# Output weights in longer runs, mixed earlier, and other cuts of three loads, in a decode layer of attention and a dense block

## The chip, the cores and the metric

The kernel runs on one core of one Trainium2 chip. The metric is the device time of one execution in microseconds (us), lower is better; the median of seven executions is given. A core has TensorE (PE, matrix products into PSUM; PEld is its weight load), VectorE (DVE), ScalarE (ACT), GpSimd (POOL), SyncE (SP, which here only issues loads) and 16 DMA engines between HBM and SBUF. Each engine runs its own list of instructions in order and waits on semaphores.

## The reference

One decode step for two sequences. `x` is normalised; attention of 16 query heads over 8 key/value heads looks at the last 4096 cached positions; a dense block with the mish activation stands beside it; both are added to `x`.

```python
B, Sq, D = 2, 1, 448;  Hq, Hkv, Sk, Dh = 16, 8, 32768, 256;  F = 1792
xn = layernorm(x)
q = (xn @ wq) as 16 heads;  k, v = caches[:, :, Sk - 4096:, :], each for two query heads
p = softmax(q . k * Dh ** -0.5);  attention = (p @ v) as one row of 4096 @ wo
h = xn @ w1 + b1;  act = h * tanh(log(1 + exp(h)))
out = x + attention + act @ w2
```

All is bf16. The caches that are read hold 2 x 8 x 4096 x 256 elements each, 33.6 MB for keys and as much for values; the weights are wq 3.7 MB, wo 3.7 MB, w1 and w2 1.6 MB each. Nothing is read twice: some 77.7 MB in all.

## The kernel before

The order of instructions on every engine is the order of the program (a manual schedule); the framework adds the semaphores. SP issues all the large loads, in program order on one DMA queue. ACT issues x and b1 at the start on another queue.

The work is in four units `u`. A unit has four pairs (sequence, key/value head), `J = 4`, and its keys and values come in four loads each, `k(u, r)` and `v(u, g)`, 128 partitions of 16384 bytes (2 MB). Three buffers hold keys, four hold values (wq and w1 use the value buffers first, w2 a key buffer at the end). `load_wo(u)` (L104) brings the unit's output weights, 0.92 MB, as two loads with runs of 1792 bytes. The framework gives loads eight completion semaphores in turn, so a load also waits for the one eight places before it.

For a unit, DVE turns each key load (`turn`, L243, two transposes of 32x32 blocks a load) into `kt`. When all four are turned, PE makes the scores in two halves (`scores`, L318), ACT takes the exponential, DVE transposes it to `p`; `weigh` (L343) sums it for the denominator; `values` (L365) multiplies p with the value loads into `pv`; `gather` (L379, L385) copies `pv` to SBUF and sums its parts by fixed selection matrices; `finish` (L412) divides and leaves `oT`, the attention output with the head dimension on partitions, two columns (the sequences) for each of four heads and two halves. `mix(u)` multiplies oT with wo and adds to the accumulator `acc`: 8 groups of rows, each as four products of 112 columns into four groups of PSUM rows (`add_rows`, L223). In the loop `mix(u - 1)` stands after `weigh(u)`.

`acc` holds the sum of everything: it begins with x (L212), gets the mixes of four units and the dense block's second product (`dense_out`, also through `add_rows`). Query projection, the dense block's first product (`dense_in`, L443) and `mish` run ahead of the loop. In the last unit the loads are, in SP's order: wo(3), v(3,0) to v(3,2), v(3,3) in two parts of 24 and 8 tokens a partition, and w2 in three parts: its first half, then 5 rows and 2 rows of 7 of the second half (a row is 448 numbers a partition). The last value load takes another way, straight into the gathered sum (`values_fixed`, L400). After the last w2 part come its products, four copies out of acc (L559, L561) and the store of the result.

Of the kernel before, what the change touches and what calls it, by code (L numbers as in the profile page):

```python
# [11 lines left out]
BF16 = mybir.dt.bfloat16  # L12
FP32 = mybir.dt.float32
PSUM = bass.MemoryType.PSUM
# [3 lines left out]
def kernel(  # L18
# [27 lines left out]
    KU = J // Bsz  # L46
    U = Hkv // KU
    C = P // J
    CT = W // C
    T = CT // R  # L50
# [8 lines left out]
    NI = F2 // P  # L59
    DG = D // G  # L60
# [11 lines left out]
    consts = ctx.enter_context(tc.tile_pool(name="consts", bufs=1))  # L72
    small = ctx.enter_context(tc.tile_pool(name="small", bufs=2))
# [2 lines left out]
    ps_o = ctx.enter_context(tc.tile_pool(name="ps_o", bufs=1, space=PSUM))  # L76
    ps_den = ctx.enter_context(tc.tile_pool(name="ps_den", bufs=1, space=PSUM))
    ps_a = ctx.enter_context(tc.tile_pool(name="ps_a", bufs=1, space=PSUM))
    ps_m = ctx.enter_context(tc.tile_pool(name="ps_m", bufs=2, space=PSUM))

    KE = T * Dh
    kview = A_k_cache.rearrange("b (k u) s d -> u (b k) s d", u=U)
# [2 lines left out]
    def ring(name):  # L85
        return v_pool.tile([P, KE], BF16, tag="v", name=name)

    k_t, v_t, wo_t = {}, {}, {}

    def load_k(u, r):  # L90
        t = k_pool.tile([P, KE], BF16, tag="k", name="k")
        src = kview[u][:, s0:, :].rearrange("j (c t) d -> c j (t d)", c=C)
        nc.sync.dma_start(out=t[:], in_=src[:, :, r * KE : (r + 1) * KE])  # L93
        k_t[u, r] = t

    def load_v(u, g, lo=0, hi=T):
        if lo == 0:
            v_t[u, g] = ring("v")
        t = v_t[u, g]
        src = vview[u][:, s0:, :].rearrange("j (g x t) d -> g x j (t d)", g=G, x=C)  # L100
        nc.sync.dma_start(  # L101
            out=t[:, lo * Dh : hi * Dh], in_=src[g, :, :, lo * Dh : hi * Dh]
        )

    def load_wo(u):
        w = wo_pool.tile([P, KU, rep, 2 * D], BF16, tag="wo", name="wo")
        for k2 in range(KU):
            r0 = (u + U * k2) * rep * Dh
            nc.sync.dma_start(  # L109
                out=w[:, k2, :, :],  # L110
                in_=A_wo[r0 : r0 + rep * Dh, :].rearrange("(h p c) d -> p h (c d)", h=rep, p=P),
            )
        wo_t[u] = w

    x_bf = consts.tile([Bsz, D], BF16)
    nc.scalar.dma_start(out=x_bf[:, :], in_=A_x.flatten_outer_dims())
    b1_sb = consts.tile([P, 2, NI], BF16)
    nc.scalar.dma_start(out=b1_sb[:], in_=B_b1.rearrange("(k q c) -> q k c", k=2, q=P))

    load_k(0, 0)  # L120
    load_k(0, 1)
# [2 lines left out]
    for lo, hi in ((0, 4), (4, NS)):  # L124
        t = ring("wq")
# [4 lines left out]
    ident = consts.tile([P, P], BF16)  # L130
# [2 lines left out]
    nc.gpsimd.memset(qd[:], 0.0)  # L133
    ones = consts.tile([P, P], BF16)
    nc.gpsimd.memset(ones[:], 1.0)
    eps_t = consts.tile([Bsz, 1], FP32)
    nc.vector.memset(eps_t[:], 1e-5)

# [6 lines left out]
        out=rstd[:], in_=mv[:, 1:2], func=ACT.Sqrt, bias=eps_t[:], scale=1.0  # L145
# [4 lines left out]
        out=xn_bf[:],  # L150
# [8 lines left out]
        out=parm[:], in_=ident[:].rearrange("p (a o) -> p o a", o=2), axis=AXIS.X, op=ALU.add  # L159
# [3 lines left out]
        out=jm[:],  # L163
        in_=ident[:].rearrange("p (a j h) -> p j a h", j=J, h=rep),
# [4 lines left out]
        out=jm[:], in0=jm[:], scalar1=-1.0, scalar2=29952.0, op0=ALU.add, op1=ALU.mult  # L169
# [3 lines left out]
        out=mneg[:], in_=jm[:].unsqueeze(1).to_broadcast([P, TH * 8, J])  # L173
    )
    sel = consts.tile([P, 2, NQ], FP32)
    for x in range(2):
        for w in range(4):
            at = 32 * w + (2 * (w % 2) + x) * NQ
            src = ident[:, at : at + NQ]
            if w == 0:  # L180
                nc.vector.tensor_copy(out=sel[:, x, :], in_=src)
            else:
                nc.vector.tensor_tensor(
                    out=sel[:, x, :], in0=sel[:, x, :], in1=src, op=ALU.add
                )

    xr_ps = ps_m.tile([P, NS, Bsz], BF16, tag="m", name="xr_ps")
    xn_v = xn_bf[:].rearrange("b (a k) -> b a k", k=NS)
    for s in range(NS):
        r = s // 2  # L190
        step = 3 + s % 2
        xrow = consts.tile([Bsz, P // 2, 2], BF16, name=f"xrow{s}")
        nc.vector.tensor_copy(out=xrow[:], in_=xn_v[:, :, r : r + step + 1 : step])  # L193
        nc.tensor.transpose(  # L194
            xr_ps[:, s, :], xrow[:].rearrange("b a o -> b (a o)"), ident[0:Bsz, 0:Bsz]
        )
    xs = consts.tile([P, NS, 32], BF16)
    nc.gpsimd.memset(xs[:], 0.0)
    for odd in range(2):
        for half in range(2):  # L200
            o = (half + odd) % 2
            nc.vector.tensor_scalar(
                out=xs[:, odd::2, half * Bsz : (half + 1) * Bsz],
# [3 lines left out]
                op0=ALU.mult,  # L207
            )

    acc = ps_a.tile([P, DG], FP32)  # L210
    for g in range(G):
        nc.tensor.matmul(  # L212
            acc[32 * g : 32 * (g + 1), :],
            lhsT=ident[0:Bsz, 0:32],
            rhs=x_bf[:, g * DG : (g + 1) * DG],
            start=True,
            stop=False,
            skip_group_check=True,
        )

    def add_rows(lhsT, rows, stop=False):
        for g in range(G):
            nc.tensor.matmul(  # L223
                acc[32 * g : 32 * g + Bsz, :],
                lhsT=lhsT,
                rhs=rows[:, g * DG : (g + 1) * DG],
                start=False,
                stop=stop,
                skip_group_check=True,
            )  # L230
# [74 lines left out]
    def scores(u, i):  # L305
        sc = ps_sc.tile([P, TH, 32], FP32, tag="sc", name="sc")
        nc.tensor.matmul(  # L307
            sc[:].rearrange("p t m -> p (t m)"),
            lhsT=ident[:],
            rhs=mneg[:].rearrange("p a j -> p (a j)"),  # L310
            start=True,
            stop=False,
            skip_group_check=True,
        )
        for n in range(NB):
            for e in range(2):
# [16 lines left out]
        nc.vector.transpose(  # L333
            out=p_t[i][:].rearrange("p g t q -> p t g q"),
            in_=ex[:].rearrange("p t (g q) -> p t g q", g=G),
        )

    state = {}
# [70 lines left out]
    def finish(u):  # L409
# [8 lines left out]
        )  # L418
        state["oT", u] = oT

    def mix(u):
        oT, w = state.pop(("oT", u)), wo_t.pop(u)
        for k2 in range(KU):
            for h in range(rep):
                for c in range(2):
                    add_rows(oT[:, c, k2 * rep + h, :], w[:, k2, h, c * D : (c + 1) * D])
# [47 lines left out]
        nc.vector.tensor_tensor(out=t_sb[:], in0=t_sb[:], in1=den[:], op=ALU.mult)  # L474
        nc.vector.tensor_tensor(out=act_bf[:], in0=h_sb[:], in1=t_sb[:], op=ALU.mult)

    w2_parts = ((0, 0, NI), (1, 0, 5), (1, 5, NI))

    def load_w2(part):
        if part == 0:  # L480
            state["w2"] = k_pool.tile([P, KE], BF16, tag="k", name="w2")
        k, lo, hi = w2_parts[part]
        w2_in = B_w2.flatten().rearrange("(k p e) -> k p e", k=2, p=P)
        at = k * NI * D
        nc.sync.dma_start(
            out=state["w2"][:, at + lo * D : at + hi * D],
            in_=w2_in[k, :, lo * D : hi * D],
        )
# [9 lines left out]
    def turns(u, r):  # L498
        for i in range(NH):
            turn(u, r, i)  # L500
# [10 lines left out]
    for u in range(U):  # L511
        last = u == U - 1
        if last:
            load_wo(u)
        load_v(u, 0)
        load_v(u, 1)
        load_v(u, 2)
        if last:
            load_v(u, 3, 0, 24)
            load_v(u, 3, 24, T)  # L520
            for part in range(3):
                load_w2(part)
        else:
            load_v(u, 3)
            load_k(u + 1, 0)
            load_k(u + 1, 1)
            load_k(u + 1, 2)
            load_wo(u)
            load_k(u + 1, 3)
        scores(u, 0)  # L530
        scores(u, 1)
        weigh(u)
        if u > 0:
            mix(u - 1)
        for g in range(G - 1):
            values(u, g)
        if not last:
            values(u, G - 1)
            turns(u + 1, 0)
            turns(u + 1, 1)  # L540
            gather(u)
            finish(u)
            turns(u + 1, 2)
            turns(u + 1, 3)
    u = U - 1
# [2 lines left out]
    values_fixed(u, G - 1, 24, T)  # L548
    finish(u)
    mix(u)  # L550
    for part in range(3):
        dense_out(part)

    res = consts.tile([Bsz, D], BF16)
    for g in range(G):
        dst = res[:, g * DG : (g + 1) * DG]
        src = acc[32 * g : 32 * g + Bsz, :]
# [35 lines left out]
```

The softmax here doesn't subtract the row's maximum and nothing guards it: scores larger than these inputs give would overflow.

## Time and profile before

| What | us |
|---|---|
| median of 7 executions (lowest, highest) | 193.06 (192.77, 193.27) |
| the profiled execution | 193.09 |
| its span on the core | 191.3 |
| busy: PE / DVE / ACT / POOL | 68.8 / 90.7 / 11.3 / 2.9 |
| key transposes on DVE (L243), 32 | 72.1 |
| PE idle ahead of the scores (L318) | 62.4 |

The span runs from the first instruction to the last; 1.8 us of the execution lie around it. The page divides the span into 40 slices of 4.8 us and gives the busy share of each engine in tenths, so a row of nines is an engine at work throughout. A time to landing is from the issue of a load to its completion semaphore. In a line of a view in order of time the first number is the start, the second the duration in us, and the brackets give how long the engine stood idle before and what ended that. The trace also has a record of every DMA packet (start, duration, size) and of each engine's completion mark for a load, without the number of the engine.

The loads as the page lists them:

```profile
k<-in_A_k_cache_dram SPq DMA_DIRECT2D x16, 2048.0 KB, 27.3
v<-in_A_v_cache_dram SPq DMA_DIRECT2D x15, 2048.0 KB, 23.5
wo<-in_A_wo_dram SPq DMA_DIRECT2D x8, 448.0 KB, 30.5
```

### The profile page before, as it was taken

The numbers are of one execution on the slowest core, as the hardware profiler recorded it, in microseconds if no ns is written. First come the engines' busy times: TensorE is split into PE (matmuls) and PEld (weight loads), VectorE is DVE, ScalarE is ACT, GpSimd is POOL, SyncE is SP. The second block draws the span as 40 slices with busy tenths as digits, with TensorE's granted clock in tenths as the row PEclk, the third lists the DMA queues.
The fourth block names the chain that finished last, engine by engine and source line by source line (L and its number), as shares of the span: only waits on it lengthen the run. The fifth ranks groups of instructions, "written<-read, shape, count | busy, mean of one in ns | idle before, by whom it ended". The sixth has DMA issues, their size and how long they took to land.

```text
span 191.3 us, 2051 instructions
## 1 busy us (share of the span) xinstructions
PE 68.8 (36%) x892; PEld 33.7 (18%) x892; DVE 90.7 (47%) x96; ACT 11.3 (6%) x19; POOL 2.9 (2%) x13
## 2 busy tenths in 40 slices
PE   0201525197336000097234000385262000673492
PEld 0100115032113000033013000132031000231191
DVE  4897066573001998553004995822007994740001
ACT  3000030011001000011000000020010000020101
POOL 6000000000000000000000000000000000000000
PEclk9999999999755555569955555589755555599555
DMA  5999999999999999999999999999999999999980
GB/s 216 405 425 422 434 423 447 418 428 418 435 432 432 421 400 421 438 432 432 418 421 432 435 408 425 421 425 432 432 428 428 406 420 403 437 425 421 413 344 16
DMA packets 8082, 77.80 MB, mean 407 GB/s; under 512 B 1029, under 2 KB 3209, under 8 KB 3593
## 3 DMA queue, kind: packets, MB, share of 16 engines
q1 hardware_dynamic: 7796, 77.66, 96.7%
q8 instruction: 7, 0.11, 0.2%
q10 hardware_dynamic: 276, 0.01, 0.1%
q14 instruction: 3, 0.02, 0.0%
HBM read 77.67 MB, written 0.00 MB: 406 GB/s over the span
## 4 chain that ended last, share of the span: by engine, by line
DMA 86%; DVE 7%; SPq 2%; PE 2%; issue 0%; DVEq 0%
DMA k<-in_A_k_cache_dram 53%; DMA w<-in_B_w_dram 27%; DVE kt L243 7%; DMA wo<-in_A_wo_dram 7%; PE h_ps L443 1%; SPq L93 1%; SPq L126 1%; PE acc L223 0%; SPq L101 0%; DVEq L588 0%; DVE res L559 0%; SPq L109 0%
## 5 line engine op out<-in xcount | busy, mean ns | idle before, releaser
L243 DVE STREAM_TRANSPOSE kt<-k 128x2048 f32<-128x2048 f32 x32 | 72.1, 2290 | 55.8 <-DMA k<-in_A_k_cache_dram 55.8
L318 PE MATMUL sc<-kt,qd 128*32 128x512 bf16 x256 | 22.6, 511 | 62.4 <-DVE kt L243 62.4
L365 PE MATMUL pv<-v,p 128*32 128x512 bf16 x240 | 19.4, 462 | 23.7 <-DMA v<-in_A_v_cache_dram 23.7
L318 PEld LDWEIGHTS <-qd 128*32 128x32 bf16 x256 | 8.7, 117 | 74.5 <-issue 72.4
L365 PEld LDWEIGHTS <-p 128*32 128x32 bf16 x240 | 7.1, 107 | 34.2 <-issue 30.7
L333 DVE STREAM_TRANSPOSE p<-ex 128x512 bf16<-128x512 bf16 x8 | 5.7, 711 | 13.6 <-ACT ex L327 13.6
L327 ACT ACTIVATE ex<-sc 128x512 bf16<-128x512 f32 x8 | 4.8, 597 | 84.7 <-PE sc L318 84.7
L385 PE MATMUL o<-sel,vs 128*128 128x8 f32 x32 | 7.5, 364 | 2.9 <-ACT vs L379 2.9
L385 PEld LDWEIGHTS o<-sel,vs 128*128 128x128 f32 x32 | 7.1, 326 | 6.5 <-ACT vs L379 6.5
L265 PE MATMUL q_ps<-wq,xs 128*32 128x512 bf16 x28 | 3.4, 624 | 12.5 <-DMA wq<-in_A_wq_dram 12.5
L412 DVE TENSOR_TENSOR oT<-o,rec 128x16 bf16<-128x16 f32 x4 | 0.6, 145 | 12.8 <-PE o L400 12.8
L379 ACT COPY vs<-pv 128x512 f32<-128x512 f32 x4 | 2.3, 585 | 49.0 <-PE pv L365 49.0
L343 PE MATMUL dn<-p,ones 128*128 128x512 bf16 x8 | 3.1, 383 | 4.5 <-DVE p L333 4.5
L443 PE MATMUL h_ps<-xs,w 128*128 128x4 bf16 x49 | 2.8, 193 | 5.1 <-DMA w<-in_B_w_dram 5.1
L307 PE MATMUL sc<-mneg,ident 128*128 128x512 bf16 x8 | 4.3, 535 | 0.0
L282 DVE COPY qT<-qt_ps 128x16 bf16<-128x16 bf16 x4 | 0.4, 168 | 6.9 <-PE qt_ps L277 6.9
L351 DVE TENSOR_REDUCE rec<-dn 128x8 f32<-128x512 f32 x4 | 2.8, 691 | 1.9 <-PE dn L343 1.9
L443 PEld LDWEIGHTS <-w 128*128 128x128 bf16 x49 | 2.7, 152 | 5.2 <-DMA w<-in_B_w_dram 5.2
L265 PEld LDWEIGHTS <-xs 128*32 128x32 bf16 x28 | 1.0, 125 | 14.0 <-issue 14.0
L194 PE MATMUL xr_ps<-ident,xrow 2*128 2x2 bf16 x7 | 1.0, 181 | 6.5 <-DVE xrow L193 6.5
L223 PEld LDWEIGHTS <-oT 128*2 128x2 bf16 x128 | 1.8, 91 | 5.5 <-issue 5.1
L223 PE MATMUL acc<-wo,oT 128*2 128x112 bf16 x128 | 2.6, 232 | 0.3 <-DVE oT L412 0.3
(51 smaller groups left out, 28.7 us busy)
## 6 DMA issues: line engine op xcount, KB each, us to landing
k<-in_A_k_cache_dram SPq DMA_DIRECT2D x16, 2048.0 KB, 27.3
v<-in_A_v_cache_dram SPq DMA_DIRECT2D x15, 2048.0 KB, 23.5
wo<-in_A_wo_dram SPq DMA_DIRECT2D x8, 448.0 KB, 30.5
wq<-in_A_wq_dram SPq DMA_DIRECT2D x1, 2048.0 KB, 16.3
w<-in_B_w_dram SPq DMA_DIRECT2D x1, 1568.0 KB, 26.7
wq<-in_A_wq_dram SPq DMA_DIRECT2D x1, 1536.0 KB, 19.3
v<-in_A_v_cache_dram SPq DMA_DIRECT2D x1, 1536.0 KB, 26.8
w<-in_B_w_dram SPq DMA_DIRECT2D x1, 784.0 KB, 23.9
```

Source lines behind the costliest of these rows:

```text
L223: nc.tensor.matmul(acc[32 * g : 32 * g + Bsz, :], lhsT=lhsT, rhs=rows[:, g * DG : (g + 1) * DG], start=False, stop=stop, skip_group_check= ...
L243: nc.vector.transpose(out=kt[i][:, :, :, r, :], in_=t[:, i * w : (i + 1) * w].bitcast(FP32).rearrange("p (a c j) -> p a c j", c=P // (R * ...
L265: nc.tensor.matmul(q_ps[32 * u : 32 * (u + 1), :], lhsT=xs[:, s, :], rhs=wq_t[s][:, u * 512 : (u + 1) * 512], start=(s == 0), stop=(s == N ...
L307: nc.tensor.matmul(sc[:].rearrange("p t m -> p (t m)"), lhsT=ident[:], rhs=mneg[:].rearrange("p a j -> p (a j)"), start=True, stop=False, ...
L318: nc.tensor.matmul(sc[32 * w : 32 * (w + 1), :, :], lhsT=qd[:, u, 2 * n + e, :, :].rearrange("p g q -> p (g q)"), rhs=ktm[i][:, n, e, :, 3 ...
L327: nc.scalar.activation(out=ex[:].rearrange("p t m -> p (t m)"), in_=sc[:].rearrange("p t m -> p (t m)"), func=ACT.Exp, scale=scale,)
L333: nc.vector.transpose(out=p_t[i][:].rearrange("p g t q -> p t g q"), in_=ex[:].rearrange("p t (g q) -> p t g q", g=G),)
L343: nc.tensor.matmul(dn[:].rearrange("p a q -> p (a q)"), lhsT=ones[:], rhs=p_t[i][:].rearrange("p g t q -> p (g t q)"), start=(i == 0), sto ...
L351: nc.vector.tensor_reduce(out=rec[:], in_=dn[:].rearrange("p a q -> p q a"), axis=AXIS.X, op=ALU.add)
L365: nc.tensor.matmul(pv[32 * w : 32 * (w + 1), :, :].rearrange("p x d -> p (x d)"), lhsT=p_t[a // 4][:, g, 4 * (a % 4) : 4 * (a % 4) + 4, :] ...
L385: nc.tensor.matmul(po[:, c, :], lhsT=sb[:, x, c::2], rhs=sel[:, x, :], start=(x == 0 and c == 0), stop=(last and x == 1), skip_group_check ...
L443: nc.tensor.matmul(h_ps[:, i, :, :].rearrange("p k b -> p (k b)"), lhsT=w1_v[:, s, i, :], rhs=xs[:, s, 0 : 2 * Bsz], start=(s == 0), stop= ...
```

## The change

*Output weights of units 0, 1 and 2.* `load_wo` brings them in one load with 7168 bytes a partition: eight successive rows of wo lie on one partition. The unit's 1024 rows are (head group k, head h, row within the head), so a partition now stands for 8 rows of one k and h, and oT no longer fits. `relay(u)` re-lays it: 16 products with constant one-hot matrices (`hot`, made on POOL at the start) bring the 1024 values into a PSUM tile of 128 partitions by 8 rows by 2 sequences; ACT copies it to SBUF as `ox`. `mix_early(u)` then makes 8 products of full width, 448 columns, into a new accumulator `early` that begins with x. Both stand ahead of the scores of the next unit; the `mix` after `weigh` is gone. Before the last unit's scores, `carry` copies `early` to SBUF and starts `acc` from it with four fp32 products. Unit 3 keeps its two loads and `mix`.

*v(3,0).* Its first 26 tokens of each partition's 32 come in one load, the last 6 in four loads of 32 partitions each.

*w2.* Its second half comes in 4, 2 and 1 rows in place of 5 and 2.

*b1.* ACT issues it in five parts of 64, 16, 16, 16 and 16 partitions in place of one.

*Memory.* A PSUM bank goes to `early`, so the pool of small PSUM tiles has one buffer in place of two; the rows of x that are transposed at the start (`xrows`) share a buffer with `ex`.

```diff
-    ps_m = ctx.enter_context(tc.tile_pool(name="ps_m", bufs=2, space=PSUM))
+    ps_e = ctx.enter_context(tc.tile_pool(name="ps_e", bufs=1, space=PSUM))
+    ps_m = ctx.enter_context(tc.tile_pool(name="ps_m", bufs=1, space=PSUM))
...
-    def load_v(u, g, lo=0, hi=T):
+    def load_v(u, g, lo=0, hi=T, x0=0, x1=C):
...
-            out=t[:, lo * Dh : hi * Dh], in_=src[g, :, :, lo * Dh : hi * Dh]
+            out=t[J * x0 : J * x1, lo * Dh : hi * Dh], in_=src[g, x0:x1, :, lo * Dh : hi * Dh]
...
-        for k2 in range(KU):
+        if u < U - 1:
+            nc.sync.dma_start(
+                out=w[:].rearrange("p k h e -> p (k h e)"),
+                in_=A_wo.rearrange("(k u y i) d -> u y k (i d)", k=KU, u=U, i=8)[u],
+            )
+        for k2 in range(KU if u == U - 1 else 0):
...
-    nc.scalar.dma_start(out=b1_sb[:], in_=B_b1.rearrange("(k q c) -> q k c", k=2, q=P))
+    for lo, hi in ((0, 64), (64, 80), (80, 96), (96, 112), (112, P)):
+        nc.scalar.dma_start(out=b1_sb[lo:hi], in_=b1_in[lo:hi])
...
+    early = ps_e.tile([Bsz, D], FP32)
+    nc.tensor.matmul(
+        early[:], lhsT=ident[0:Bsz, 0:Bsz], rhs=x_bf[:], start=True, stop=False
+    )
     acc = ps_a.tile([P, DG], FP32)
...
+    def carry():
+        e_sb = small.tile([P, 2 * Dh], FP32, tag="vs", name="e_sb", bufs=1)[0:Bsz, 0:D]
+        nc.scalar.copy(out=e_sb, in_=early[:])
+        for g in range(G):
+            nc.tensor.matmul(
+                acc[32 * g : 32 * g + Bsz, :],
+                lhsT=id2[:],
+                rhs=e_sb[:, g * DG : (g + 1) * DG],
+                start=True,
...
+    def relay(u):
+        oT = state.pop(("oT", u))
+        ox_ps = ps_m.tile([P, 4, 2, Bsz], FP32, tag="m", name="ox_ps")
+        for h in range(rep):
+            rows = slice(h * 64, (h + 1) * 64)
+            for y in range(4):
+                for k in range(KU):
+                    nc.tensor.matmul(
+                        ox_ps[rows, y, :, :],
+                        lhsT=hot[:, k, y, :, :].rearrange("p q k -> p (q k)"),
+                        rhs=oT[:, :, k * rep + h, :],
...
+    def mix_early(u):
+        ox = state.pop(("ox", u))
+        w = wo_t.pop(u)[:].rearrange("p k h (c d) -> p (k h c) d", c=2)
+        for i in range(8):
+            nc.tensor.matmul(
+                early[:],
+                lhsT=ox[:, i, :],
+                rhs=w[:, i, :],
...
-    w2_parts = ((0, 0, NI), (1, 0, 5), (1, 5, NI))
+    w2_parts = ((0, 0, NI), (1, 0, 4), (1, 4, 6), (1, 6, NI))
...
-        load_v(u, 0)
+        if last:
+            load_v(u, 0, 0, 26)
+            for x0 in range(0, C, 8):
+                load_v(u, 0, 26, T, x0, x0 + 8)
+        else:
+            load_v(u, 0)
...
+        if u > 0:
+            relay(u - 1)
+            mix_early(u - 1)
+        if last:
+            carry()
         scores(u, 0)
         scores(u, 1)
         weigh(u)
-        if u > 0:
-            mix(u - 1)
```

More of the change, by code (lines that the diff above doesn't have):

```diff
@@ L94, in load_k @@
         k_t[u, r] = t
-    def load_v(u, g, lo=0, hi=T):
-        if lo == 0:
+    def load_v(u, g, lo=0, hi=T, x0=0, x1=C):
+        if lo == 0 and x0 == 0:
             v_t[u, g] = ring("v")
@@ L117 @@
     b1_sb = consts.tile([P, 2, NI], BF16)
-    nc.scalar.dma_start(out=b1_sb[:], in_=B_b1.rearrange("(k q c) -> q k c", k=2, q=P))
+    b1_in = B_b1.rearrange("(k q c) -> q k c", k=2, q=P)
+    for lo, hi in ((0, 64), (64, 80), (80, 96), (96, 112), (112, P)):
+        nc.scalar.dma_start(out=b1_sb[lo:hi], in_=b1_in[lo:hi])
     load_k(0, 0)
@@ L135 @@
     nc.gpsimd.memset(ones[:], 1.0)
+    id2 = consts.tile([Bsz, Bsz], FP32)
+    nc.vector.tensor_copy(out=id2[:], in_=ident[0:Bsz, 0:Bsz])
+    hot = consts.tile([P, KU, 4, 32, KU], BF16)
+    nc.gpsimd.memset(hot[:], 0.0)
+    for k in range(KU):
+        nc.gpsimd.tensor_copy(
+            out=hot[:, k, :, :, k], in_=ident[:].rearrange("p (q y) -> p y q", y=4)
+        )
     eps_t = consts.tile([Bsz, 1], FP32)
@@ L191 @@
         step = 3 + s % 2
-        xrow = consts.tile([Bsz, P // 2, 2], BF16, name=f"xrow{s}")
-        nc.vector.tensor_copy(out=xrow[:], in_=xn_v[:, :, r : r + step + 1 : step])
+        if s % 4 == 0:
+            xrows = small.tile([P, 4, P // 2, 2], BF16, tag="ex", name="xrows")
+        xrow = xrows[0:Bsz, s % 4, :, :]
+        nc.vector.tensor_copy(out=xrow, in_=xn_v[:, :, r : r + step + 1 : step])
         nc.tensor.transpose(
-            xr_ps[:, s, :], xrow[:].rearrange("b a o -> b (a o)"), ident[0:Bsz, 0:Bsz]
+            xr_ps[:, s, :], xrow.rearrange("b a o -> b (a o)"), ident[0:Bsz, 0:Bsz]
         )
@@ L208 @@
             )
+    early = ps_e.tile([Bsz, D], FP32)
+    nc.tensor.matmul(
+        early[:], lhsT=ident[0:Bsz, 0:Bsz], rhs=x_bf[:], start=True, stop=False
+    )
     acc = ps_a.tile([P, DG], FP32)
[L211 to L219, printed above, removed]
+    def carry():
[7 more added lines that the diff above has]
+                start=True,
+                stop=False,
+                skip_group_check=True,
+            )
     def add_rows(lhsT, rows, stop=False):
@@ L419, in finish @@
         state["oT", u] = oT
+    def relay(u):
[4 more added lines that the diff above has]
+            for y in range(4):
+                for k in range(KU):
+                    nc.tensor.matmul(
+                        ox_ps[rows, y, :, :],
+                        lhsT=hot[:, k, y, :, :].rearrange("p q k -> p (q k)"),
+                        rhs=oT[:, :, k * rep + h, :],
+                        start=(y == 0 and k == 0),
+                        stop=(y == 3 and k == KU - 1),
+                        skip_group_check=True,
+                    )
+        ox = small.tile([P, 8, Bsz], BF16, tag="ox", name="ox")
+        nc.scalar.copy(
+            out=ox[:].rearrange("p i b -> p (i b)"),
+            in_=ox_ps[:].rearrange("p y c b -> p (y c b)"),
+        )
+        state["ox", u] = ox
+    def mix_early(u):
[6 more added lines that the diff above has]
+                rhs=w[:, i, :],
+                start=False,
+                stop=(u == U - 2 and i == 7),
+            )
     def mix(u):
@@ L520 @@
             load_v(u, 3, 24, T)
-            for part in range(3):
+            for part in range(len(w2_parts)):
                 load_w2(part)
@@ L550 @@
     mix(u)
-    for part in range(3):
+    for part in range(len(w2_parts)):
         dense_out(part)
```

## The prediction

> **What bounds the kernel now.** I read the page's slices and queue table first, then the chain that ended last, then two tables of stages, and last the order in time at the end and at the start.
>
> ```profile
> DMA  5999999999999999999999999999999999999980
> ...
> DMA packets 8082, 77.80 MB, mean 407 GB/s; under 512 B 1029, under 2 KB 3209, under 8 KB 3593
> ...
> q1 hardware_dynamic: 7796, 77.66, 96.7%
> ...
> DMA 86%; DVE 7%; SPq 2%; PE 2%; issue 0%; DVEq 0%
> ```
>
> The 16 DMA engines are busy from the second slice to the last but one, and SP's queue alone fills them for 96.7% of the span. The time is a stream of loads, a head of 2 us and a tail after the last load; no compute engine is above 47%. So what counts is what makes bytes dearer, and what lets the 16 engines finish unevenly.
>
> ```profile
> 68.50:71.20 2.70, 0.00 (x0) 0.00 (x0) 2.38 (x3) 0.00 (x0) 0.00 (x0) 0.50 0.99 375
> ...
> 40.00:60.00 20.00, 12.29 (x121) 4.63 (x113) 3.69 (x11) 2.01 (x4) 0.00 (x0) 0.77 1.00 426
> ```
> ```profile
> 183.00:185.00 2.00, 2.00 (x67) 2.00 (x66) 0.00 (x0) 0.00 (x0) 0.00 (x0) 0.50 0.96 386
> 185.00:187.00 2.00, 1.70 (x65) 1.43 (x63) 0.18 (x1) 0.00 (x0) 0.00 (x0) 0.50 0.48 189
> ```
>
> The last two columns are the DMA engines' share and GB/s. While unit 0's output weights stream (first line) the engines are as busy as ever but move 375 GB/s; with k and v alone 426. In the last 2 us only 0.48 of them work: half have finished. The packet records of the trace, which these views sum up, say it sharper. Of the 16 completion marks of the last w2 load nine come between 184.9 and 185.7 us and seven between 186.5 and 187.2. The late engines fell back one at a time: each instruction fetch (the q8 row of the page, 7 packets of 16 KB) occupies one engine and sets it back by about 1.55 us (the last two, near the end, by less), a new engine each time. Followed from packet to packet, the fetches take the engines that were 10th, 11th, 12th and so on to start the first load. If that order is their number, these are engines 9 to 14, all in the upper half. A seventh engine, seemingly of the lower half, lost 1.0 us to four slow 1792-byte packets.
>
> ```profile
> 178.92 1.90 PE L365 MATMUL pv<-v,p 128*32 128x512 bf16 x16 [3.84 <-DMA v<-in_A_v_cache_dram]
> ...
> 187.13 0.92 PE L223 MATMUL acc<-w,act_bf 128*2 128x112 bf16 x28 [0.16 <-DMA w<-in_B_w_dram]
> ```
> ```profile
> b_sb<-in_B_b_dram ACTq DMA_DIRECT2D x1, 3.5 KB, 12.8
> ```
>
> PE waits for loads at both points of the end: what comes after 187.13 is 20 products of the middle w2 part (landed 187.13) and 8 of the last part, which landed at 187.65 (its mark plus 0.4).
>
> [...] the median 1792-byte packet holds its engine 75 ns, a 16384-byte one 614; the slope is 539 ns / 14592 B = 0.037 ns per byte, so 1792 B alone would be 66 and each packet costs some 9 more. [...] Every 128-partition load here leaves 16 marks, the two-row x load 2[...]. [...] 3.5 KB take 12.8 us, because 16 packets of 14 bytes an engine each wait for one 0.61 us packet of SP's queue (16 x 0.61 = 9.8, and 3 to start). [...]
>
> **The change part by part.**
>
> *Output weights, units 0 to 2.* Before, an engine moves 32 packets of 1792 B a unit; its marks say 2.47 us (68.71 to 71.18 on the fastest engine). After, 8 packets of 7168 B, each 75 + 5376 x 0.037 = 273 ns, 2.18 us. The saving a unit is 0.22 by packet lengths, 0.29 by marks; 0.32 by the GB/s (2.7 us x 51/426). Three units: 0.66 to 0.96. I take 0.80, on all engines.
>
> *Six tokens of v(3,0).* The main load has 13312-byte runs: 113 ns less each, 8 an engine, -0.90 on all. The rest comes as four loads of 32 partitions, whose slowest source dimension is 8. [...] 16 packets of 3072 B (122 ns) each: +1.95. Lower half +1.05, upper half -0.90; marks add 0.04 to the lower.
>
> *w2 in four parts.* Runs of 3584, 1792 and 896 B in place of 4480 and 1792: one packet more for each of 8 partitions, 8 x 9 ns, and a mark: +0.08. After the last landing 4 products remain in place of 8: at 23 ns apart, -0.09.
>
> *Sum per engine.* Lower half: -0.80 + 1.05 + 0.04 + 0.08 = +0.37. Upper half: -0.80 - 0.90 + 0.08 = -1.62. The last packets of the early group, 185.7, become 186.05; those of the late upper group, 187.2, become 185.6. The lower half now ends last, at 186.05: 1.17 us earlier. (The slow seventh engine I take for a chance of those short packets.) With the tail, -1.25.
>
> *PE's own path to the end.* It starts at v(3,2)'s landing (178.92) and needs 8.05 us to the end of the first w2 part. All engines have done the same moves by then, so v(3,2) lands some 1.2 us earlier too; the rest, 28 products in 0.95, ends near 186.7, and the last landing plus 4 products is near 186.8. PE does not take over, but only by a tenth or so.
>
> *Relay, mix_early, carry.* Each unit gets 16 one-hot products (at most 188 ns, the qr_ps row: 3.0), a 128x16 ACT copy (0.25, as res) and 8 products 448 wide (at most 511 ns, the row of the scores: 4.1); it loses 32 narrow ones (0.6). They stand ahead of scores, where PE idles for DVE's turns 62.4 us in four waits. The tightest is the last: wo(2) lands at 156.8 and scores start at 164.18. mix_early 4.1, e_sb copy 0.6, four fp32 products 1.5 (364 ns each): 6.2 of 7.4. Queued behind is scores(3); an overrun up to 1.2 us would still be covered by PE's 1.25 us wait for v(3,1) at 174.03. Cost nothing. The mix that leaves 171.34 only lengthens that wait.
>
> *b1 in five loads.* ACT issues four more (0.41 each), so the square root and DVE's prelude come 1.7 to 2 us later: the first turn starts near 10.3 in place of 8.5, the second ends near 19.3; DVE's next need is at 24.88. Nothing. But the loads take eight semaphores in turn, each waiting for the one eight before it; with four more ahead, the changed program makes SP's second wq load, k(0,2), w1, k(0,3), v(0,0) wait for one b1 part each. The first part has 8 packets an engine, so lands near 1.3 + 3 + 9 x 0.61 = 9.8, the others 3 turns (1.85) later each: 11.7, 13.5, 15.4, 17.2. What is queued before (k(0,0), k(0,1), wq) keeps the engines busy to about 17.5, and every load after is worth 3.7 us or more. Even if the first part took as long as all of b1 before (14.1), wq's data would start at 16. Nothing; between nothing and, if starved, the gap itself.
>
> *SP at the end.* v(3,1) now waits for k(3,3), v(3,2) and v(3,3) for wo(3) and v(3,0), w2 for the four small loads. At k(3,3)'s landing (161.8 before) wo(3) and v(3,0), 3.0 MB or 7 us, are still queued, about 5 on the engine furthest ahead; issue and start take 2. No gap. The new POOL work (`hot`) is before 5 us, DVE's id2 copy waits only for ident (1.30).
>
> **Sum.** Profiled execution 193.09 (span 191.3 and 1.8 around it) - 1.25 = 191.84; the median is 0.03 lower: 191.8.
>
> **The rivals.**
>
> 1. *Ports shared.* Two of the four small loads go to partitions 64 to 127[...]. [...] those 8 packets (0.97 us) take twice as long and the upper engine loses the 0.9 it was spared. Lower half +1.34, end 187.05; upper -0.72, end 186.5. Total -0.25: 192.8. [...]
>
> 2. *No half.* The small loads spread over 16 engines. Then every engine keeps its bytes and gains 0.80 less 0.15: the late group ends at 186.6, 192.4.
>
> 3. *The wrong half (slower).* The late engines are numbered 0 to 7, because starting order is not number. Their 187.2 gets +0.37, with shared ports +1.34: 193.4 to 194.4, middle 193.8. It decides from the point where one engine that a fetch hit before 183 us lies in the lower half. Against: six successive fetches hit six successive places of that order, the 10th to the 15th, which a random numbering would not give.
>
> That the weights' runs would not get longer I rule out by the source: 8 rows of 448 lie together.
>
> **How the numbers follow.** Forecast 0.55 (191.4 to 192.2), ports 0.20 (192.4 to 193.0), no half 0.10 (192.1 to 192.6), wrong half 0.09, a start that starves or an unseen wait 0.06. The range 191.3 to 193.0 holds the first three. Within 0.2% means 192.67 to 193.45, what a measurement can tell from no change. Faster: 0.55 + 0.10 + about half of the ports' case = 0.76. Same: the other half and the mild end of the wrong half, 0.14. Slower: 0.10.
>
> **What would show it.** Right: the stretch of wo near 68 to 71 us at 410 GB/s or more; in the last 2 us before the final w2 landing a DMA share near 0.9 in place of 0.48; last w2 landing near 186.4; PE's wait before scores never zero. Ports: the same share near 0.9 but packets of 3072 B far above 122 ns, and a landing after 187. Wrong half: the last 2 us at a share below 0.5. A DMA slice below 9 in the first 20 us would say that the b1 waits starve the stream.

## The result and the profile after

| Kernel | median us | lowest to highest | executions |
|---|---|---|---|
| before | 193.07 | 192.77 to 193.31 | 30 |
| after | 194.69 | 193.82 to 194.97 | 12 |

The ratio is 1.0076, with a 95% interval from 1.0066 to 1.0085: the change makes the kernel 1.6 us slower. The forecast was 191.8 and faster. The executions of after stand in two groups, three from 193.82 to 194.03 and nine from 194.48 to 194.97; the profiled one is the fastest of all (193.82, span 192.0), so its lines show the loss rather too small.

The slices, the queues and the chain on the page of after:

```profile
DMA  5999999999999999999999999999999999999980
GB/s 219 427 410 420 437 428 449 413 418 427 433 433 423 430 421 433 430 423 420 427 433 427 417 439 427 433 423 420 433 427 423 417 443 406 345 396 427 410 329 10
DMA packets 7249, 77.80 MB, mean 405 GB/s; under 512 B 1092, under 2 KB 1864, under 8 KB 2760
...
q1 hardware_dynamic: 6900, 77.66, 96.4%
q8 instruction: 7, 0.11, 0.2%
...
q14 instruction: 2, 0.02, 0.0%
...
DMA 76%; DVE 11%; PE 5%; issue 3%; ACTq 2%; ACT 1%; SPq 0%; DVEq 0%
```

The engines are as busy as before, with 833 packets fewer, yet the mean rate fell from 407 to 405 GB/s. The row of rates says where: 345 in slice 35 (163.2 to 168.0 us), the lowest of all but the first and the last two. PE's share of the chain rose from 2 to 5%.

The table of stages of after (us; busy time of PE, PEld, DVE, ACT, POOL; PE clock, DMA share, GB/s):

```profile
68.50:71.20 2.70, 0.42 (x12) 0.42 (x12) 2.37 (x3) 0.00 (x0) 0.00 (x0) 0.50 1.01 421
40.00:60.00 20.00, 12.37 (x121) 4.70 (x113) 3.63 (x11) 2.01 (x4) 0.00 (x0) 0.77 1.01 430
164.00:168.00 4.00, 4.00 (x49) 1.46 (x45) 1.86 (x2) 0.60 (x1) 0.00 (x0) 0.65 1.07 343
...
183.00:185.00 2.00, 2.00 (x37) 2.00 (x37) 0.00 (x0) 0.00 (x0) 0.00 (x0) 0.50 1.03 416
185.00:187.00 2.00, 1.73 (x72) 1.65 (x73) 0.17 (x1) 0.00 (x0) 0.00 (x0) 0.50 0.65 251
```

The first line is the forecast come true: output weights at 421 GB/s in place of 375, close to the 430 of k and v alone in the second. The last two look like the better balance that was forecast, 0.65 of the engines at work at the end in place of 0.48; the completion marks below say otherwise. The third line is the price: while the six tokens move (164 to 168 us) the engines are full (1.07) and deliver 343 GB/s. Before had this there:

```profile
164.00:168.00 4.00, 3.82 (x41) 1.49 (x44) 2.32 (x2) 0.60 (x1) 0.00 (x0) 0.66 1.03 434
```

PE in order of time at the end of after (start, duration, group, idle time before and what ended it):

```profile
174.95 1.90 PE L391 MATMUL pv<-v,p 128*32 128x512 bf16 x16 [3.10 <-DMA v<-in_A_v_cache_dram]
179.85 1.90 PE L391 MATMUL pv<-v,p 128*32 128x512 bf16 x16 [3.00 <-DMA v<-in_A_v_cache_dram]
182.49 1.87 PE L411 MATMUL o<-sel,vs 128*128 128x8 f32 x8 [0.74 <-ACT vs L405]
184.21 1.85 PE L426 MATMUL o<-p,v 128*128 128x8 bf16 x64
186.33 0.91 PE L249 MATMUL acc<-wo,oT 128*2 128x112 bf16 x32 [0.27 <-DVE oT L438]
187.03 1.82 PE L249 MATMUL acc<-w,act_bf 128*2 128x112 bf16 x56
```

The products of v(3,1) start at 174.95, where before has 174.03, and those of v(3,2) on its landing at 179.85, 0.93 us later than before, where it was forecast some 1.2 earlier. From there PE has no gap that a load would explain: the 56 products of w2 run through. So in this execution PE's path from v(3,2) sets the end. The last w2 load is close behind: it landed at 188.55, 0.3 us before PE's last product ended.

### The profile page after: what moved, and what is told of

Read it like the earlier page. It is cut to its first block, busy times and chain, and to the rows that moved or that the text cites. A ratio compares the mean times of both kernels' runs of the same rounds, so it can differ in the third digit from the quotient of the medians.

```text
span 192.0 us, 2032 instructions
## 1 busy us (share of the span) xinstructions
PE 82.4 (43%) x873; PEld 38.1 (20%) x873; DVE 91.3 (48%) x97; ACT 12.3 (6%) x23; POOL 3.9 (2%) x16
## 4 chain that ended last, share of the span: by engine, by line
DMA 76%; DVE 11%; PE 5%; issue 3%; ACTq 2%; ACT 1%; SPq 0%; DVEq 0%
DMA k<-in_A_k_cache_dram 60%; DVE kt L269 9%; DMA v<-in_A_v_cache_dram 9%; DMA wo<-in_A_wo_dram 7%; ACTq L126 1%; PE acc L249 1%; PE pv L391 1%; PE o L411 1%; PE o L426 1%; ACT L160 1%; DVE sel L199 1%; PE xr_ps L212 1%; DVE xs L220 0%; ACT vs L405 0%; SPq L94 0%
## 5 line engine op out<-in xcount | busy, mean ns | idle before, releaser
L391 PE MATMUL pv<-v,p 128*32 128x512 bf16 x240 | 20.3, 478 | 24.8 <-DMA v<-in_A_v_cache_dram 24.8
L344 PE MATMUL sc<-kt,qd 128*32 128x512 bf16 x256 | 23.3, 522 | 13.5 <-DVE kt L269 13.5
L454 PE MATMUL ox_ps<-oT,hot 128*64 128x4 bf16 x48 | 2.3, 192 | 29.8 <-DVE oT L438 29.8
L473 PE MATMUL early<-wo,ox 128*2 128x448 bf16 x24 | 9.4, 572 | 5.1 <-DMA wo<-in_A_wo_dram 5.1
L454 PEld LDWEIGHTS <-hot 128*64 128x64 bf16 x48 | 2.5, 151 | 29.8 <-issue 29.7
L212 PE MATMUL xr_ps<-ident,xrows 2*128 2x2 bf16 x7 | 1.0, 181 | 9.0 <-DVE xrows L211 9.0
L473 PEld LDWEIGHTS <-ox 128*2 128x2 bf16 x24 | 2.8, 115 | 9.6 <-issue 8.5
```

The costliest lines, as they stand in the source:

```text
L344: nc.tensor.matmul(sc[32 * w : 32 * (w + 1), :, :], lhsT=qd[:, u, 2 * n + e, :, :].rearrange("p g q -> p (g q)"), rhs=ktm[i][:, n, e, :, 3 ...
L391: nc.tensor.matmul(pv[32 * w : 32 * (w + 1), :, :].rearrange("p x d -> p (x d)"), lhsT=p_t[a // 4][:, g, 4 * (a % 4) : 4 * (a % 4) + 4, :] ...
L454: nc.tensor.matmul(ox_ps[rows, y, :, :], lhsT=hot[:, k, y, :, :].rearrange("p q k -> p (q k)"), rhs=oT[:, :, k * rep + h, :], start=(y == ...
L473: nc.tensor.matmul(early[:], lhsT=ox[:, i, :], rhs=w[:, i, :], start=False, stop=(u == U - 2 and i == 7),)
```

## The experiments

The theory at the start, called the ports theory in the expectations: four small loads (each leaves eight completion marks in after, a large one sixteen) are dear where they write to partitions 64 to 127, for the engines that bring them and for the others. That ports lie behind it was the author's assumption; no run shows them. The rivals: the number of small loads (issues, marks, waits), the cut as such, b1's five loads at the start, or the new path over relay and `early`. All runs side by side:

| Run | what it is | median us | ratio to before (95%) |
|---|---|---|---|
| e1_no_six | after, v(3,0) whole | 192.89 | 0.9988 (0.9981 to 0.9995) |
| e2_six_even | after, the six tokens in one load | 192.91 | 0.9987 (0.9981 to 0.9994) |
| e3_before_six | before, with the cut of v(3,0) alone | 194.89 | 1.0087 (1.0073 to 1.0101) |
| e4_b1_one | after, b1 whole | 195.07 | 1.0098 (1.0085 to 1.0112) |
| e5_own_ports | e3, small loads to partitions 0 to 63 only | 192.47 | 0.9966 (0.9955 to 0.9978) |
| e6_other_ports | e3, small loads to partitions 64 to 127 only | 194.27 | 1.0057 (1.0044 to 1.007) |
| e7_no_six_b1_one | after, v(3,0) and b1 whole | 192.53 | 0.9965 (0.9952 to 0.9979) |
| e8_wo_only | before, with the output weights' part alone | 192.83 | 0.9987 (0.998 to 0.9993) |
| e9_pad_w2 | e7, 32 more small products on PE | 191.78 | 0.9931 (0.9917 to 0.9944) |
| e10_pad | e8, the same 32 | 192.51 | 0.9965 (0.9953 to 0.9978) |
| e11_after_pad | after, the same 32 | 194.71 | 1.0082 (1.0068 to 1.0096) |
| e12_two_tokens | e3, two tokens in place of six | 193.14 | 1.0004 (0.9995 to 1.0012) |

The median of before was 193.08 to 193.23 in these comparisons.

### Which part costs the time

*e1_no_six* takes the cut of v(3,0) out of after:

```diff
-        if last:
-            load_v(u, 0, 0, 26)
-            for x0 in range(0, C, 8):
-                load_v(u, 0, 26, T, x0, x0 + 8)
-        else:
-            load_v(u, 0)
+        load_v(u, 0)
```

> The changed kernel with v(3,0) in one load. Ports theory[...]: the loss of about 1 us at 165 to 170 us of the span goes, the weights' saving stays: 192.2 to 192.7, below before. Rival (the relay, the early mix or the b1 waits cost the time): 194 or more, as the changed kernel.

*e2_six_even* keeps the cut, but brings the six tokens in one load of 128 partitions:

```diff
-            for x0 in range(0, C, 8):
-                load_v(u, 0, 26, T, x0, x0 + 8)
+            load_v(u, 0, 26, T)
```

> The changed kernel with the six tokens in one load of 128 partitions in place of four of 32: the same cut, the same runs of 3072 bytes[...]. Ports theory: within 0.2 of the kernel without the cut, 192.3 to 192.9. If the cut itself (more packets, later completion of v(3,0), waits of SP on the small loads) costs the time: 194 or more.

*e3_before_six* puts the cut, and nothing else, into before:

```diff
-        load_v(u, 0)
+        if last:
+            load_v(u, 0, 0, 26)
+            for x0 in range(0, C, 8):
+                load_v(u, 0, 26, T, x0, x0 + 8)
+        else:
+            load_v(u, 0)
```

> The kernel before with only the cut of v(3,0) into 26 tokens and four loads of 6. Ports theory: slower than before by 1.5 to 2.5 us, 194.6 to 195.6, since the lower engines end about 2 us later. Rival (the rest of the change costs the time): within 0.4 of 193.07.

*e4_b1_one* gives after its b1 back in one load:

```diff
-    for lo, hi in ((0, 64), (64, 80), (80, 96), (96, 112), (112, P)):
-        nc.scalar.dma_start(out=b1_sb[lo:hi], in_=b1_in[lo:hi])
+    nc.scalar.dma_start(out=b1_sb[:], in_=b1_in)
```

> The changed kernel with b1 in one load. If the five parts are hidden, as forecast: within 0.3 of the changed kernel's 194.69. Rival (the waits on b1 parts at the start delay the stream): 0.5 us or more below it.

Measured: without the cut 192.89, which is 1.80 us less than after; with the cut alone 194.89, which is 1.8 more than before. The same amount both ways: the whole loss is the cut of v(3,0). It isn't the extra load or the short packets, for the cut in one load costs nothing (192.91 beside 192.89). It isn't b1: whole, after was slower still. What is left is that the load is split by partitions. (192.89 and 195.07 are 0.2 and 0.1 us above what was expected.)

### What makes the split dear

*e5_own_ports* is e3 with two of the four small loads, those of partitions 0 to 63. It leaves out part of the computation: the last six tokens of v(3,0) on partitions 64 to 127 are set to zero instead of loaded.

```diff
-            for x0 in range(0, C, 8):
+            for x0 in (0, 8):
                 load_v(u, 0, 26, T, x0, x0 + 8)
+            nc.gpsimd.memset(v_t[u, 0][64:128, 26 * Dh :], 0.0)
```

> The kernel before with v(3,0) cut, and of the four small loads only the two of partitions 0 to 63; the six tokens of partitions 64 to 127 are not loaded but set to zero on POOL, so 0.2 MB less is read. [...] Ports theory: the packets of 3072 bytes stay at 0.12 us, the upper engines are spared 0.9 us, so the end comes earlier: 192.0 to 192.7. If small loads on eight engines cost time by themselves: 194 or more.

*e6_other_ports* is its mirror: the loads of partitions 64 to 127 stay, and the six tokens of partitions 0 to 63 are set to zero.

```diff
-            for x0 in range(0, C, 8):
+            for x0 in (16, 24):
                 load_v(u, 0, 26, T, x0, x0 + 8)
+            nc.gpsimd.memset(v_t[u, 0][0:64, 26 * Dh :], 0.0)
```

> The same with the two small loads of partitions 64 to 127 in place of those of 0 to 63 (which are set to zero)[...]. Ports theory: the packets take about 0.24 us, both halves lose 0.9 us against the run with partitions 0 to 63: 0.8 to 1.8 us slower than that one, 193.0 to 194.2. Without an effect of the port: the same time as that one within 0.3.

The two kernels move the same bytes in the same number of packets from as many issues; only the partitions that are written differ, and with them the part of v(3,0) that is read. They are 1.80 us apart, 192.47 and 194.27, the second 0.1 above its expected range. The table of stages of e5:

```profile
164.00:168.00 4.00, 3.82 (x33) 1.30 (x32) 2.31 (x2) 0.17 (x1) 0.00 (x0) 0.50 1.03 434
```

and of e6:

```profile
164.00:168.00 4.00, 3.91 (x37) 1.35 (x40) 2.23 (x2) 0.26 (x1) 0.00 (x0) 0.55 1.03 331
```

Both have full engines (1.03), but one gets 434 GB/s out of them and the other 331. The packet records, by size, in us:

```
kernel            3072-byte packets: count, lowest, median, mean, highest
e2_six_even       128   0.121  0.121  0.123  0.133
e5_own_ports       64   0.121  0.121  0.122  0.129
e6_other_ports     64   0.121  0.233  0.196  0.264
e3_before_six     128   0.121  0.147  0.173  0.254
after             128   0.121  0.124  0.166  0.271
```

A packet into partitions 64 to 127 takes about twice as long (a median of 0.233 us in e6 beside 0.121 in e5), and the others pay too: of the 62 packets of 16384 bytes that begin between 166 and 170 us in after, 27 took over 0.70 us, up to 1.19, where 0.61 is normal; in before one of 98 did. Why the partition matters isn't shown: which engine wrote which partition the trace doesn't tell.

*e12_two_tokens* asks whether the bytes or the loads cost. It is e3 with two tokens in the four small loads in place of six, so a third of the bytes:

```diff
-            load_v(u, 0, 0, 26)
+            load_v(u, 0, 0, 30)
             for x0 in range(0, C, 8):
-                load_v(u, 0, 26, T, x0, x0 + 8)
+                load_v(u, 0, 30, T, x0, x0 + 8)
```

> The kernel before with only the last two tokens of v(3,0), not six, in the four small loads (1024-byte packets, a third of the bytes, as many loads, instructions and marks). If the port's bytes cost the time: a third of the +1.8 us that six tokens cost, +0.3 to +0.8 us, 193.4 to 193.9. If four small loads cost a fixed time (issues, marks, waits): +1.5 to +2, 194.6 to 195, as with six tokens.

Measured 193.14, no difference from before: outside both forecasts, but a fixed cost of 1.5 us for four small loads is ruled out. (By its trace e12 is not quite even with before. Its last w2 load lands at 188.08, before's at 187.65, and the time from the landing of the store to the end of the span is 0.96 us in place of 1.44.) The tables of e12 and of e3 over the longer stretch, where before has 413 GB/s at a share of 0.98, e12 first:

```profile
165.00:170.00 5.00, 5.00 (x53) 1.65 (x49) 2.15 (x2) 0.60 (x1) 0.00 (x0) 0.56 1.02 387
```
```profile
165.00:170.00 5.00, 5.00 (x57) 1.65 (x49) 1.62 (x2) 0.60 (x1) 0.00 (x0) 0.60 1.06 321
```

The lost rate does go by the bytes: 26 GB/s for two tokens, 92 for six. Over 5 us, at 430 GB/s, that is 0.3 and 1.1 us of stream. Each of the eight engines without small loads is spared 0.9 us by six tokens, the prediction's term (eight packets with 0.502 us for 13312 bytes in after in place of 0.614 for 16384 in before), and by two tokens a third of that, 0.3 by estimate. So two tokens come out even, and six should cost some 0.2 by this count; they cost 1.8. Such a count is a mean over the engines, and a load lands with its last one. From e3:

```profile
181.19 1.90 PE L365 MATMUL pv<-v,p 128*32 128x512 bf16 x16 [2.98 <-DMA v<-in_A_v_cache_dram]
```

v(3,2) lands 2.27 us later than the 178.92 of before; in e12 it is 179.27, 0.35 later. The completion marks show the same: the 16 marks of v(3,1) spread over 2.2 us before, 2.4 in e12, 3.4 in after and 3.5 in e3, and in after the last of them stands alone, 1.24 us behind the fifteenth (174.44 and 173.20).

Which engine is this? The packet records don't carry its number, but a small load leaves eight marks, read here as one for each engine, the same eight for all four loads: in after each of the four has seven marks close together and one 1.31 to 1.58 us behind. The marks of the first small load, as they reach its semaphore (some 0.4 us after the mark):

```
kernel          early                     late                      profiled execution, us
after           165.85 to 166.16 (7)      167.47                    193.82
e5_own_ports    166.59 to 167.09 (7)      168.23                    192.63
e3_before_six   166.68 to 167.08 (6)      168.63, 169.03            194.88
e11_after_pad   166.02 to 166.22 (6)      167.85, 168.85            194.99
e4_b1_one       165.90 to 166.33 (5)      168.24, 168.50, 168.55    195.04
```

In each of these five profiles at least one of the eight engines was late when the small loads began, even in e5, where no packet was slow. Its lag is older. Each of the 14 profiles has, in its first 100 us, one instruction packet of 8 KB on a second queue, q14, that takes an engine 0.33 to 0.36 us: at 39.8 to 40.3 us in the kernels with the long runs of wo, at 69.8 to 70.2 in the others. The next packets on that engine, read as those that begin where it ends (40.39 us in after, 70.32 in before), are slow too, one of 16384 bytes with 1.27 us in place of 0.61, or four of 1792 bytes with 0.20 to 0.25 in place of 0.075. From then on one more engine is 0.9 to 1.4 us behind the others at every load. In after its mark of v(3,0)'s first 26 tokens comes at 166.58, between ten early ones (165.38 to 165.93) and the five that a fetch on q8 had hit (from 167.66; q8 had five fetches in the span by then, 1.06 to 1.10 us each). It is the late one of the eight: four small packets, the longest of which is 0.271 us, lead from 166.58 to 167.47, but from no other of these marks.

The rest of the loss is even. In e1, without the cut, ten marks of v(3,1) reach the semaphore from 171.24 to 171.64 and six from 172.63 to 173.03. In after three are left from 171.50 to 171.83, twelve come from 172.99 to 173.77 and the last at 174.91. So, counting marks, the seven early engines with small loads lost about 1.9 us and the three without about 0.25. The prediction's rival *Ports shared* had 1.05 + 0.97 and -0.90 + 0.9. What makes the time worse than the mean is that the small loads went, among others, to an engine that was 1 us late already.

Only one engine takes the packet on q14, so where two or three of the eight are late, a fetch on q8 had by this count hit one or two of them. Those profiled executions took 194.88 to 195.04, that of after with one late engine 193.82. This suggests why the executions of after fall in two groups; without profiles of the slower ones it isn't shown.

### Where the saving of the output weights goes

*e7_no_six_b1_one* and *e8_wo_only* strip the change down: e7 is after with v(3,0) and b1 whole; e8 has also w2 in three parts again, so that only the long runs, relay and the early mix are left. What e8 changes beyond e7:

```diff
-    w2_parts = ((0, 0, NI), (1, 0, 4), (1, 4, 6), (1, 6, NI))
+    w2_parts = ((0, 0, NI), (1, 0, 5), (1, 5, NI))
```

> The changed kernel with v(3,0) in one load and b1 in one load: what is left is the weights' longer runs with the relay, and w2 in four parts. If the five b1 parts are neutral: 192.89 within 0.15. If they help, as in the changed kernel, where one load was 0.4 slower: 193.1 to 193.3.

> The kernel before with the weights' longer runs, relay and early mix alone. By the sum of the forecast: 0.7 to 0.9 below before, 192.3. By what the kernel without the cut of v(3,0) showed, where the same part was in: 192.9 to 193.2, most of the saving lost after the last landing.

Measured 192.53 and 192.83, both outside what was expected. In e8 the last completion mark of w2 is at 186.18, where before has 187.23: the stream is 1.05 us shorter, a little more than the 0.80 of the forecast. But the time fell by 0.30. PE at the end of e8:

```profile
185.14 0.86 PE L248 MATMUL acc<-w,act_bf 128*2 128x112 bf16 x28
186.18 0.62 PE L248 MATMUL acc<-w,act_bf 128*2 128x112 bf16 x17 [0.18 <-DMA w<-in_B_w_dram]
187.26 0.45 PE L248 MATMUL acc<-w,act_bf 128*2 128x112 bf16 x11 [0.46 <-issue]
```

After 45 of the 56 products PE stands still for 0.46 us and then goes on. No load can be the reason: the next part of w2 begins with product 49. In the chain of e8 this gap is a piece called "issue" (186.80, 0.46). The same gap stands after the same product in e1 (0.19 us), e7 (0.36) and e2:

```profile
187.37 0.45 PE L249 MATMUL acc<-w,act_bf 128*2 128x112 bf16 x11 [0.60 <-issue]
```

The instruction queue q8 gives a candidate: before has its sixth instruction fetch at 182.69, e8 at 184.82. The change takes some twenty products and as many weight loads off PE's list (892 of each on the page of before, 872 or 873 on that of e8), so that the last products stand at an earlier place in it. In these four profiles the sixth fetch begins between 184.42 and 185.09, and PE goes on 2.3 to 2.5 us after its begin.

*e9_pad_w2* and *e10_pad* test that: they make the one-hot products of units 0 and 1 a second time, 32 useless products far ahead of the end, in e7 and e8. They only shift PE's list.

```diff
-        for h in range(rep):
+        for h in (0, 1, 0, 1) if u < 2 else (0, 1):
```

> The kernel with the weights' longer runs, w2 in four parts, v(3,0) and b1 in one load (192.53), and 32 pairs of weight load and product more on PE: the relay's products of units 0 and 1 are made twice, where PE idles. If PE's pause after the 44th w2 product is a wait for its instructions, whose place in the program the 52 instructions fewer have moved to the end, the pause goes: 0.3 to 0.6 faster, 192.0 to 192.3. If the pause is a wait for the load: no change, 192.4 to 192.7.

> The same 32 pairs more in the kernel with the weights' longer runs alone (192.83; its second w2 load has landed before the pause). Instructions theory: the pause of 0.46 us and the quarter of a microsecond outside the span go, 192.1 to 192.5. Rival (the pause is the load's, or more PE work costs time): 192.8 or more.

*e11_after_pad* does the same to after.

> The same 32 pairs more in the changed kernel (194.69). There PE's chain and the last landing end together, so instructions theory: 0 to 0.6 faster, 194.1 to 194.7; the loss by the four small loads stays, so above 193.8 in any case.

Measured: e10 is 0.32 us below e8, e9 is 0.75 below e7 (0.2 us beyond the expected range), and at 191.78 it is the fastest of all kernels here, 1.45 below before. PE at the end of e9:

```profile
185.42 1.87 PE L248 MATMUL acc<-w,act_bf 128*2 128x112 bf16 x56
```

and of e10:

```profile
185.61 1.89 PE L248 MATMUL acc<-w,act_bf 128*2 128x112 bf16 x56
```

All 56 products in one piece: more work on PE, and an earlier end. The sixth fetch is at 177.16 in e9. A second part of the gain lies outside the span: the profiled execution of e7 takes 192.48 for a span of 190.4 (2.05 outside), that of e9 191.75 for 190.0 (1.77), and before, after, e9 and e10 have seven fetches on the page, e1, e2, e7 and e8 six. That the pause hangs on the place in PE's list is shown; that the fetch is what PE waits for is inferred from the times.

In after the same pad gains nothing (194.71). Its trace has no such pause: the sixth fetch begins at 184.79, and PE, which had waited for v(3,2), reaches its last eleven weight loads only at 188.29.

## Why the prediction was wrong

*Output weights: right.* -0.80 was forecast. From mark to mark a unit's weights take the fastest engine 2.17 us in place of 2.47, the rate is 421 in place of 375, and alone (e8) the stream ends 1.05 earlier. Why the last engines gain more than 0.80 isn't shown; the ten early marks of v(3,1) come only 0.6 to 0.8 earlier.

*Six tokens of v(3,0): the step that failed.* The forecast was "Lower half +1.05, upper half -0.90". "Lower half" are the eight engines that run the small loads, "upper half" the other eight; which numbers they have no trace shows. That the loads take eight engines, 16 packets each, was an assumption of the author's; it held (in after eight marks each, and 128 packets of 3072 bytes in all), and so did the forecast that partitions 0 to 63 cost nothing extra: e5's packets took 0.122 us. The sum went wrong at two terms.

The first is the partitions from 64 on, which the sum put at nothing and left to the rival *Ports shared*, at 192.8. Its packets of twice the time are what e5 and e6 show (0.121 and 0.233 us); its shared ports are not shown. The lost rate is of its size: 103 GB/s for 4 us is 0.41 MB, or 0.96 us at 430 GB/s, where it had 0.97.

The second is "The slow seventh engine I take for a chance of those short packets". It was no chance: behind the packet on q14 an engine is late in every profile, with long runs of wo too, and where the marks decide it (after, e3, e5, e11, e12) it is one of the eight that run the small loads. Its 1 us adds to theirs. In after fifteen marks of the last w2 load come by 186.95, where *Ports shared* had 187.05 for the lower half; the sixteenth, alone as at every load since v(3,1), comes at 188.14. v(3,2) came 0.93 us (after) to 2.27 us (e3) later than before.

Together the cut measured +1.8 (after over e1, e3 over before). The sum had counted it at -0.43: without it the late group would have ended at 187.2 - 0.72 = 186.48, with it the end was 186.05. That is 2.2 of the 2.85 us between forecast and result.

The rival of the wrong half is not ruled out for every execution. e5 is 0.66 below before, which speaks against it (e5 leaves half of these bytes out, so it's no measure of the gain). But its test was whether an engine that a fetch had hit lies in the lower half, and in e3, e4 and e11 one or two of the eight engines are, by the count above, such ones.

*"PE does not take over, but only by a tenth or so": wrong, twice.* With the cut, v(3,2) lands late and PE's path from there sets the end in the profiled execution of after. Without it, the w2 loads land early enough, and then PE's pause of 0.19 to 0.60 us in the last products takes part of the gain. Without the cut the same sum gives some 192.3, and e1 measured 192.89. The pause in its profile (0.19) and the longer part outside the span (2.05 in place of 1.78) are 0.46 of that; the rest was not followed up.

*w2 in four parts: under-sized.* Forecast -0.01 in sum (+0.08 and -0.09). Measured -0.30 (e7 under e8) and -0.73 (e9 under e10). Why it is worth so much more was not tried; single executions of e7 lie as far apart as 191.99 and 192.86.

*b1 in five loads: not settled.* Forecast nothing. Of the start that holds: the first slices run at 219, 427, 410, 420 GB/s, so nothing starves, and DVE's first turn begins at 10.64 (10.3 forecast). But five loads help by 0.38 beside one with the cut (194.69 and 195.07) and cost 0.36 without it (192.89 and 192.53). Signs that change with the rest of the kernel point to a shift of which engine is late (three of the eight in e4's profile, one in that of after); what sets it was not tested.

*Relay, mix_early, carry: hidden, as forecast.* The time line of after ahead of the last scores:

```profile
153.48 0.78 PE L454 MATMUL ox_ps<-oT,hot 128*64 128x4 bf16 x16 [9.88 <-DVE oT L438]
...
155.96 3.15 PE L473 MATMUL early<-wo,ox 128*2 128x448 bf16 x8 [1.70 <-DMA wo<-in_A_wo_dram]
...
159.77 0.55 PE L238 MATMUL acc<-e_sb,id 2*2 2x112 f32 x8 [0.67 <-ACT e_sb L236]
...
163.21 1.05 PE L344 MATMUL sc<-kt,qd 128*32 128x512 bf16 x8 [2.35 <-DVE kt L269]
```

PE still waits 2.35 us for DVE after all of it.

*The seven late engines.* In the last two microseconds the share rose from 0.48 to 0.65, but not because the late engines finish earlier. Of the marks of the last w2 load nine came by 185.7 before and seven from 186.5 to 187.2; in after three come by 185.1, twelve from 186.26 to 186.95 and one at 188.14. The early engines were made late, and the last one later.

## What to carry to other kernels

When work is moved from one set of DMA engines to another, ask into which partitions they write. Here 3072-byte packets into partitions 64 to 127 took 0.233 us (e6), into partitions 0 to 63 0.121 (e5), and 16384-byte packets beside them up to 1.19 in place of 0.61 (after). Judge by the engine that ends last, not by the mean (0.2 us by the mean, 1.8 measured), and look for it before the change: an engine that is already late, for a reason that has nothing to do with the load (0.9 to 1.4 us behind here), should not get more. When a stream has been made shorter, look at the compute engine's list at the end: a gap with no load behind it may hang on the place in that list (0.46 us in e8), and a few harmless instructions earlier can move it away (32 products made e8 faster by 0.32 us, e7 by 0.75).

## What the runs showed of the hardware

- Small loads on eight engines, beside the large ones: 3072-byte packets into partitions 64 to 127 took 0.233 us (median, e6), into partitions 0 to 63 0.121 (e5). 16384-byte packets took up to 1.19 in place of 0.61 (after), and the core's stream fell from 434 to 331 GB/s (e5, e6) at the same share of busy engines. A share near 1 says that engines are occupied, not that bytes move.
- In all 14 profiles an 8 KB instruction packet on q14 (0.33 to 0.36 us) is followed on its engine by slow packets: one of 16384 bytes with 1.27 us, or four of 1792 bytes with 0.20 to 0.25. The engine stays about 1 us late to the end. Why the packets behind it are slow is open.
- PE paused 0.19 to 0.60 us in its last products in four profiles, and went on 2.3 to 2.5 us after the begin of an instruction fetch; 32 more products, placed elsewhere, made the kernel faster by 0.32 and 0.75 us.
- In the profiled execution of after the store of the result was issued 0.5 us after the last copy had ended (189.92 and 189.43); in before it followed at once. A fetch on q8 ended at 189.79, but e11 has the same 0.5 us (191.01 and 190.52) with that fetch over at 189.79. The cause was not tried.
